# Loads on one queue, weight pieces by columns and a new order of issue, in a gated linear attention and MLP-mixer kernel

## The chip, the cores and the metric

The kernel runs on one core of one Trainium2 chip. A core has five engines with instruction streams of their own: PE (TensorE, matrix products), DVE (VectorE), ACT (ScalarE), POOL (GpSimd) and SP (SyncE, which here only issues transfers). They meet through semaphores. Sixteen DMA engines move data for all of them. The metric is the device time of one execution in microseconds (us); an execution of the profile has a span, which the time exceeds by what lies around it.

## The reference

The inputs are q, k, v and alpha, of shape 4 x 8 x 768 x 48 (batch, heads, positions, head width), and four weights. The first part is a recurrence with a state of 48 x 48 for each batch and head, the second a mixer over tokens and channels:

```python
for t in range(S):                       # S = 768
    state = alpha[:, :, t, :, None] * state + einsum('bhd,bhe->bhde', k[:, :, t], v[:, :, t])
    y[:, :, t] = einsum('bhd,bhde->bhe', q[:, :, t], state)
...
x = y.transpose(0, 2, 1, 3).reshape(B, S, H * D)         # 4 x 768 x 384
xt = x.transpose(0, 2, 1)
h = maximum(xt @ w_tok1, 0) @ w_tok2                     # 768 -> 256 -> 768
u = x + h.transpose(0, 2, 1)
out = u + maximum(u @ w_ch1, 0) @ w_ch2                  # 384 -> 1536 -> 384
```

## The kernel before

**Chunks.** The recurrence is cut into twelve chunks n of 256 positions, three to a batch (b = n // 3, k = n % 3). A chunk is loaded as four tiles of 128 partitions x 768 numbers (names ld_at, ld_kt, ld_qt, ld_vt with the number n; a partition holds two positions next to each other, so a run of memory is 384 bytes). Its steps, with the line that the profile shows: the logarithm of alpha (ln, L586, for chunks 0 to 2; P, ln1, lnP and r1 in the others, L577 to L589), its running sum by a triangular product on PE (cumw or cum), exponentials of plus and minus that sum (E, IE, Et), k times IE (kk) and q times E (qq, both L641; in chunks from 3 on after k0a, L633, and q0r, L637, which bring one of the two positions in), a copy of v to bf16 (vb) with two shifted halves (vs0, vs1) and, from chunk 3 on, shifted copies of k (ka, kb, kc). For chunks 0 to 5 PE transposes kk and qq (trk, trq, L654), and the results are copied out of PSUM (evk, evq); for the others a DMA transpose issued by SP does it (dk, dq, L665). Then G0 and G1 (products of k and q), the masks (L708), K (the new part of the state), s0, sa and sm (the state, L750, L753, L756), ia and ib (q with the state), y0 and y1 (the mask's result with v), x0 and x1 (the copy of y: a tile of 128 positions). On PE the products cum, K, G, ia, ib, y and the unread ones all go through one helper and show as L592.

**Mixer.** For each batch: t1 (first token weight, L790) with its relu ht, t2 (second token weight, L795; each t2_b_i makes 128 columns of h, i from 0 to 5), u = x + h (L799), transposes up of u with copies ut (batches 0 and 1) or DMA transposes ux (batches 2 and 3), c1_b_mc_half (first channel weight, L814; mc is one of twelve groups of 128 columns, half one of two groups of 384 positions, three matmuls each) with its relu rt on ACT (L785) or DVE (L787), c2_b_i_q4 (second channel weight, L819, four steps of three matmuls), o = u + result (L823) and the store st (L573). Of the last tile to finish, (3, 0), c2, o and st are done in two column ranges, h0 and h1.

**Weights.** Each weight is loaded in pieces of 128 x 768 float32 numbers (ldw_wt1, ldw_wt2, ldw_wc1, ldw_wc2 with the piece's number, L549 to L556), and cast to bf16 (cw_...). A step that reads a weight waits for the casts of the pieces that are named in its preds.

**Order.** Nothing is scheduled at run time. The string ORDER lists all steps with the engine that does each (t PE, s ACT, v DVE, g POOL, y SP), and the steps are emitted in that order, so each engine works its own through in order of the list; BUFS gives the buffers in the same order. Load tiles and weight pieces share twenty buffers of a class "in", o has four, PSUM eight banks. A step waits for what it reads and for the last reader of its buffer. Loads and stores may be issued by SP or ACT. One rule more: steps of DVE and POOL that are marked port=True (kk, qq, vb, vs, sm, P, k0a, q0r, ka, kb, kc, casts, pq) wait for the last such step of the other engine in the list's order (shared, L672 to L681).

**Unread products.** In the first three chunks a step may be preceded by fillers: f1_... is one product and f3_... are three products of a tile of zeros with itself, 128 x 512, written to the PSUM bank that the step then overwrites. Nothing reads them. Which of them are done is set by whether ORDER names them.

## Time and profile before

| | |
|---|---|
| median of three runs | 167.17 us (166.69 to 168.16) |
| the profiled execution | 167.49 us |
| its span | 165.8 us |
| moved by DMA | 34.46 MB in 74,530 packets, 67,984 of them under 512 bytes |
| read from and written to HBM | 25.17 MB and 4.72 MB |

A group of the profile has its line, engine, operation, what it writes and reads, the shape and the count, then the busy time in us and the mean ns of one, then the idle time of the engine just before such instructions and what ended most of it. A row of a timeline has the start in us, the time it covers, and in brackets the idle time before it and its releaser. The forty slices are a fortieth of the span each, some 4.1 us, and a digit is the busy share in tenths.

### The profile page before, as it was taken

To read this page: it belongs to the slowest core of one execution; us is meant where nothing else is said; L and a number is where in the kernel's file an instruction comes from. 1 tells how busy PE (TensorE), PEld (TensorE's weight loads), DVE (VectorE), ACT (ScalarE), POOL (GpSimd) and SP (SyncE) were. 2 spreads that over 40 slices of the span, in tenths; PEclk is the share of its full clock that TensorE was granted. 3 is DMA by queue.
4 is the path that set the end of the run, shared out by engine and by line. 5 is a ranking of instruction groups with operands and counts; after the bars stand their busy time and mean duration, and the time that the engine had idled before them with its cause. 6 is when DMAs were issued, how large, how long until landed. Compare 5 with 4: busy or idle time off the path is not lost. (4 is left out here: it accounts for less than half of the span.)

```text
span 165.8 us, 4057 instructions
## 1 busy us (share of the span) xinstructions
PE 155.9 (94%) x1606; PEld 99.2 (60%) x1606; DVE 117.6 (71%) x205; ACT 102.6 (62%) x195; POOL 65.3 (39%) x73
## 2 busy tenths in 40 slices
PE   7956999899889999999999999999999999999992
PEld 2434666576567666765567666666566565656662
DVE  4059999999769877997978899898584751353241
ACT  3685899999699974869988882846613203453000
POOL 4045966473294926386297584233020000000000
PEclk9999999999999999999999999999999999999999
DMA  4999999999999898999988999667601044150124
GB/s 116 323 325 324 320 325 369 373 321 335 368 353 315 204 298 208 271 264 190 303 237 129 241 270 144 142 134 163 185 0 51 0 90 100 47 190 4 47 95 142
DMA packets 74530, 34.46 MB, mean 208 GB/s; under 512 B 67984, under 2 KB 73488, under 8 KB 74512
## 3 DMA queue, kind: packets, MB, share of 16 engines
q1 hardware_dynamic: 58432, 25.47, 60.4%
q10 hardware_dynamic: 16080, 8.75, 17.9%
q8 instruction: 12, 0.20, 0.5%
q14 instruction: 6, 0.05, 0.1%
HBM read 25.17 MB, written 4.72 MB: 180 GB/s over the span
## 5 line engine op out<-in xcount | busy, mean ns | idle before, releaser
L819 PE MATMUL ps<-wc,rt 128*128 128x384 bf16 (+1 forms) x300 | 53.9, 320 | 0.0
L814 PE MATMUL ps<-ut,wc 128*128 128x384 bf16 x288 | 51.4, 326 | 1.7 <-ACT rt L785 1.6
L785 ACT ACTIVATE rt<-ps 128x384 bf16<-128x384 f32 x59 | 26.7, 490 | 21.4 <-PE ps L814 19.2
L814 PEld LDWEIGHTS <-wc 128*128 128x128 bf16 x288 | 27.3, 97 | 19.4 <-issue 2.4
L819 PEld LDWEIGHTS <-rt 128*128 128x128 bf16 x300 | 27.5, 97 | 15.5
L708 DVE TENSOR_TENSOR gtm<-ps,mk 128x1024 bf16<-128x1024 f32 x24 | 28.6, 1219 | 3.9 <-PE ps L592 3.5
L787 DVE TENSOR_SCALAR rt<-ps 128x384 bf16<-128x384 f32 x37 | 19.9, 554 | 11.0 <-PE ps L814 10.9
L823 DVE TENSOR_TENSOR o<-ps,u 128x384 f32<-128x384 f32 (+1 forms) x25 | 13.1, 536 | 11.8 <-PE ps L819 9.0
L641 POOL TENSOR_TENSOR pkk<-in,IE 128x768 bf16<-128x768 f32 x7 | 12.7, 1816 | 16.3 <-DVE pkk L641 7.7
L641 POOL TENSOR_TENSOR pkq<-in,E 128x768 bf16<-128x768 f32 x7 | 12.7, 1819 | 3.2 <-DVE ss L756 1.5
L592 PE MATMUL ps<-zs 128*128 128x512 bf16 x37 | 12.3, 454 | 1.6 <-DVE zs L495 1.1
L685 ACT CAST vb<-in 64x384 bf16<-64x384 f32 (+1 forms) x20 | 12.4, 621 | 1.1 <-DMA in<-in_v_dram 0.8
L685 ACT CAST x<-ps 128x384 bf16<-128x384 f32 x18 | 8.5, 476 | 7.4 <-PE ps L592 6.9
L799 DVE TENSOR_TENSOR u<-ps,x 128x384 bf16<-128x384 f32 x24 | 11.9, 550 | 1.3 <-PE ps L795 1.0
L756 POOL TENSOR_TENSOR ss<-tmp,E 128x384 bf16<-128x384 f32 x10 | 8.3, 835 | 7.8 <-DVE tmp L753 4.6
L577 POOL TENSOR_TENSOR in<-in 128x384 f32<-128x384 f32 x7 | 7.0, 1000 | 11.1 <-DVE wt L686 3.4
L790 PE MATMUL ps<-x,wt 128*128 128x384 bf16 x48 | 10.8, 326 | 0.3 <-ACT x L685 0.3
L753 DVE TENSOR_TENSOR tmp<-ps,ss 128x384 f32<-128x384 f32 x16 | 8.8, 553 | 2.0 <-PE ps L592 1.3
L641 DVE TENSOR_TENSOR pkk<-in,IE 128x768 bf16<-128x768 f32 x5 | 4.8, 954 | 7.1 <-ACT IE L625 6.0
L592 PE MATMUL ps<-tpq,tpk 48*64 48x128 bf16 (+1 forms) x288 | 8.5, 219 | 1.0 <-DVE tpq L686 0.8
L795 PE MATMUL ps<-ht,wt 128*128 128x384 bf16 x48 | 9.3, 326 | 0.0
L592 PEld LDWEIGHTS <-gtm 128*128 128x128 bf16 x192 | 7.6, 96 | 1.9
(93 smaller groups left out, 211.2 us busy)
## 6 DMA issues: line engine op xcount, KB each, us to landing
in<-in_q_dram SPq DMA_DIRECT2D x11, 384.0 KB, 5.1
in<-in_moe_w_ch_dram SPq DMA_DIRECT2D x10, 384.0 KB, 5.9
in<-in_alpha_dram SPq DMA_DIRECT2D x9, 384.0 KB, 5.8
in<-in_k_dram SPq DMA_DIRECT2D x9, 384.0 KB, 6.4
in<-in_v_dram SPq DMA_DIRECT2D x6, 384.0 KB, 5.5
in<-in_v_dram ACTq DMA_DIRECT2D x6, 384.0 KB, 5.7
out_dram<-o ACTq DMA_DIRECT2D x12, 192.0 KB, 2.6
out_dram<-o SPq DMA_DIRECT2D x11, 192.0 KB, 2.3
```

The source lines that it names most:

```text
L592: return self.pe.matmul(out, lhsT=lhsT, rhs=rhs, start=start, stop=stop, skip_group_check=True)
L641: self.shared(self.eng[e].tensor_tensor(self.t(dst)[:, :, :, 0:D], self.t(src).rearrange("p h s d -> p s h d"), bass.AP(tensor=f.tensor, o ...
L685: return self.act.copy(d, s)
L708: self.nc.vector.tensor_tensor(self.t(gtm)[:, hf, :, :], self.pair(gp).rearrange("p a (j t) -> p (a j) t", t=128), bass.AP(tensor=m.tensor ...
L785: self.act.activation(d, s, AF.Relu)
L787: self.nc.vector.tensor_scalar_max(d, s, 0.0)
L790: self.pe.matmul(self.bank(bank)[:, 0:HD], lhsT=self.wt1[:, kc, m * 128 : m * 128 + 128], rhs=self.t(x), start=(kc == 0), stop=(kc == NS - 1))
L795: self.pe.matmul(self.bank(bank)[:, 0:HD], lhsT=self.wt2[:, kc, i * 128 : i * 128 + 128], rhs=self.t(hts[kc]), start=(kc == 0), stop=(kc = ...
L799: self.nc.vector.tensor_tensor(self.t(u)[:, i % 3], self.bank(bank)[:, 0:HD], self.t(x), ALU.add)
L814: self.pe.matmul(self.bank(bank)[:, 0:HD], lhsT=self.wc1[:, kc, mc * 128 : mc * 128 + 128], rhs=self.t(ut)[:, 3 * half : 3 * half + 3, kc, ...
L819: self.pe.matmul(self.bank(bank)[:, 0 : cz - ca], lhsT=self.t(rts[mc][0])[:, i * 128 : i * 128 + 128], rhs=self.wc2[:, mc, ca:cz], start=( ...
L823: self.nc.vector.tensor_tensor(self.t(o)[:, ca:cz], self.bank(bank)[:, 0 : cz - ca], self.t(u)[:, i % 3, ca:cz], ALU.add)
```

## The change

Five things change. The computation stays the same.

- All loads are issued by SP. Before, ACT issued sixteen of the 64 loads and thirteen of the 25 stores; now it issues three stores.
- The second token weight is loaded in two halves of 384 columns (for all 256 rows) instead of two of 128 rows, and t2_b_i waits for the half that holds its columns instead of both.
- The first channel weight is loaded in six pieces of 256 columns (for all 384 rows) instead of six of 128 rows x 768 columns, and a c1 step waits for one piece instead of three. A run of memory is 1 KB instead of 3 KB, and 1.5 KB instead of 3 KB in the second token weight.
- The list names 23 unread products instead of 37.
- ORDER and BUFS are new as a whole, and with them the engine of many steps: without transfers, ACT has 173 steps instead of 194, DVE 197 instead of 187, POOL 72 instead of 61. The two ranges of the last tile are 320 and 64 columns instead of 192 each. (The fill that cum gets is empty, as cum is used from chunk 3 on only.)

The diff, with the part of the two lists that comes up to the first steps of c1 of batch 0:

```diff
@@ -162,7 +162,8 @@
             lnp = O("lnP", act(384, True), 1, writes=[la], reads=[at], preds=[p_], emit=lambda e: g.lnp(la, at))
             r1 = O("r1", act(384, True), 3, writes=[lf], preds=[ln1], emit=lambda e: g.r1(lf))
             cb = V("one")
-            cum = O("cum", pe([384] + [4] * 4 + [16]), 2, writes=[cb, E, IE], reads=[la], preds=[lnp], emit=lambda e: g.cum(cb, la))
+            cum = O("cum", pe([384] + [4] * 4 + [16]), 2, writes=[cb, E, IE], reads=[la], preds=[lnp] + fill("cumw", cb),
+                    emit=lambda e: g.cum(cb, la))
             e1 = et = O("E", act(400), 4, writes=[E], reads=[cb], preds=[cum], emit=lambda e: g.expE(E, cb))
             e2 = O("IE", act(384), 4, writes=[IE], reads=[cb], preds=[cum], emit=lambda e: g.expIE(IE, cb))
             k_in = [O("k0a", either(dve(384), pool_tt(384)), 2, writes=[kt], reads=[at], port=True,
@@ -290,7 +291,7 @@
                 u = V("u")
             bank = V("one")
             o = P.op(f"t2_{b}_{i}", pe([384] * 2), m0 + (1900 + 330 * i) * sc, writes=[bank],
-                     reads=[h for h, _ in hts], preds=[h for _, h in hts] + [wl[("wt2", p)] for p in range(2)],
+                     reads=[h for h, _ in hts], preds=[h for _, h in hts] + [wl[("wt2", i // 3)]],
                      emit=lambda e, i=i, bank=bank: g.tok2(bank, i, [h for h, _ in hts]))
             uo = P.op(f"u_{b}_{i}", dve(384), m0 + (1950 + 330 * i) * sc, writes=[u], reads=[bank, x[i][0]], preds=[o],
                       emit=lambda e, i=i, bank=bank, u=u: g.uadd(u, i, bank, x[i][0]))
@@ -319,7 +320,7 @@
             for half in range(2):
                 bank = V("one")
                 o = P.op(f"c1_{b}_{mc}_{half}", pe([384] * 3), m0 + (4900 + 975 * mc + 487 * half) * sc, writes=[bank],
-                         reads=[ut], preds=(uts[0:2 + half] if b in UP else [uts[half]]) + [wl[("wc1", mc // 6 * 3 + p)] for p in range(3)],
+                         reads=[ut], preds=(uts[0:2 + half] if b in UP else [uts[half]]) + [wl[("wc1", mc // 2)]],
                          emit=lambda e, mc=mc, half=half, bank=bank: g.ch1(bank, ut, mc, half))
                 ro.append(P.op(f"rt_{b}_{mc}_{half}", either(act(384), dve(384)),
                                m0 + (4950 + 975 * mc + 487 * half) * sc, writes=[rt], reads=[bank], preds=[o],
@@ -327,7 +328,7 @@
             rts.append((rt, ro))
         for i in range(NS):
             hold = 4000.0 if (i >= NS - 3 and b < B - 1) else 0.0
-            cuts = [(0, HD // 2), (HD // 2, HD)] if (b, i) == LAST else [(0, HD)]
+            cuts = [(0, 320), (320, HD)] if (b, i) == LAST else [(0, HD)]
             for ci, (ca, cz) in enumerate(cuts):
                 nm = f"{b}_{i}" if len(cuts) == 1 else f"{b}_{i}h{ci}"
                 bank, o_ = V("one"), V("o")
@@ -361,85 +362,84 @@
 
 ENGINES = {"t": "PE", "s": "ACT", "v": "DVE", "g": "POOL", "y": "SP"}
 ORDER = """
-f1_cumw0t ld_at1y f3_cumw1t f3_trk1t ld_at0s ld_kt1s f1_cumw1t ln1s f3_trq0t ld_kt0y ld_vt0y ld_qt0y ln0s ld_vt1y
-ld_qt1y ld_at2y cumw1t f1_K1t cumw0t ld_at3y E1s IE1s Et1s IE0s vb0s f1_K0t kk0v Et0s kk1g K0t f3_K1t s0_0v sa1_0v E0s
-qq0v vb1s trk0t sm1_0v f3_G00t trq0t ln2s trk1t evk0v ld_qt2y qq1g K1t evq0v evk1s sa0_1v ld_vt2s G0_0t cumw2t
-mask0_0v sm0_1g trq1t P3g ln13s E2s vs0_1s vs1_0s qq2g ld_kt3y ld_kt2y sa1_1v Et2s evq1v lnP3s f3_y0t f3_G01t IE2s
-G1_0t mask1_0v ib0t G0_1t f1_trq2t mask0_1v trq2t cum3t ld_qt3y k0a3g vs0_0g ldw_wt10y f3_G11t y1_0t ldw_wt11y y0_0t
-G1_1t evq2s ib1t ldw_wt21s f3_trk2t kk2v E3s IE3s trk2t sm1_1g mask1_1v vb2s vs1_1s f1_K2t ld_vt3y K2t evk2v G1_2t
-ldw_wt20y y1_1t ld_at4y sa0_2v f3_G02t kk3g x1_0s r13s sm0_2g q0r3g G0_2t mask1_2v vs0_2g cw_wt10s ia1t x0_0v y0_1t
-trk3t t1_0_1_0t mask0_2v ka3s ia2t ldw_wc14y t1_0_1_1t f1_y2t ib2t y0_2t vs1_2v kb3s ldw_wc15y y1_2t x1_1s cw_wt11s
-vb3v x0_1s t1_0_1_2t t1_0_0_0t t1_0_1_3t kc3s x0_2s t1_0_1_4t vs0_3v vs1_3v ldw_wc13y x1_2s t1_0_0_1t qq3v cw_wt21s
-t1_0_0_2t t1_0_1_5t cw_wt20v t1_0_0_3t t1_0_0_4t t1_0_0_5t ht_0_1s K3t trq3t ld_kt4y ht_0_0s P4g s0_3v sa1_3v t2_0_2t
-t2_0_3t evk3s sm1_3g t2_0_0t t2_0_1t t2_0_5t ldw_wc12y ldw_wc10y ldw_wc11y u_0_3v u_0_2v u_0_0v up_0_1t t2_0_4t evq3s
-lnP4s cw_wc14g cw_wc15g u_0_1v ib3t ut_0_1s ln14s ld_kt5s u_0_5v cw_wc13g up_0_0t cum4t ld_at5y E4s G0_3t IE4s u_0_4v
-G1_3t k0a4g ut_0_0v up_0_2t c1_0_10_0t mask0_3v c1_0_9_0t ut_0_2s rt_0_10_0s rt_0_9_0s mask1_3v c1_0_7_0t c1_0_9_1t
-c1_0_6_0t c1_0_10_1t c1_0_8_0t c1_0_8_1t cw_wc12s y1_3t cw_wc10s rt_0_10_1s kk4v rt_0_7_0v cw_wc11v rt_0_6_0v trk4t
-c1_0_1_0t P5g ka4g c1_0_4_1t rt_0_8_1v c1_0_1_1t k0a5g ld_vt4s r14s x1_3s c1_0_3_1t c1_0_0_0t evk4v rt_0_1_1v
-rt_0_0_0v rt_0_8_0s ln15s ldw_wc20s lnP5s rt_0_4_1s rt_0_3_1s ld_qt4y cum5t c1_0_2_0t kc4v kb4s ldw_wc24s IE5s
-rt_0_9_1s c1_0_11_1t q0r4v qq4v c1_0_4_0t ld_vt5s rt_0_1_0s rt_0_2_0v E5s c1_0_2_1t rt_0_4_0s rt_0_11_1s kk5g
...
+f1_cumw0t f3_cumw0t ld_at0y ld_vt0y vb0v ld_at1y ln0s cumw0t ld_kt0y ld_qt0y ld_at2y ln1s IE0s f1_trq1t f1_cumw1t
+ld_at3y Et0s kk0v E0s cumw1t ld_qt1y K0t qq0v ld_vt1y IE1s ld_kt1y s0_0v sa1_0v trk0t vs1_0v ld_qt2y evk0v Et1s ln2s
+E1s vs0_0s P3g trq0t cumw2t evq0s f3_G00t f1_G10t ld_vt2y G0_0t f3_G10t IE2s lnP3s ld_kt2y f1_trk1t G1_0t qq1v sm1_0v
+mask0_0v mask1_0v Et2s ld_kt3y ldw_wt10y ld_vt3y ldw_wt20y ldw_wt11y trq1t vb1g kk1g ldw_wt21y K1t E2s y0_0t cum3t
+evq1s trk1t f3_y0t sa0_1v evk1s ln13s vs1_1s E3s IE3s qq2v sm0_1v x0_0v ld_at4y sa1_1v G0_1t mask0_1v ib0t y1_0t kk2g
+f1_trq2t G1_1t ld_qt3y trq2t ldw_wc12y r13s ld_kt4y ldw_wc14y mask1_1v vs0_1s trk2t x1_0v f1_y1t vb2s evk2v k0a3g
+sm1_1g ldw_wc15y evq2s K2t sa0_2v f3_y1t cw_wt10s G0_2t vb3s ib1t y1_1t ldw_wc10y G1_2t ia1t ia2t t1_0_1_0t mask0_2v
+t1_0_1_1t y0_1t kk3g ld_qt4y vs1_2g sm0_2g cw_wt11g cw_wt21g kb3s vs0_2s y0_2t trk3t x0_1s mask1_2v t1_0_0_0t
+t1_0_0_1t x1_1v ka3s x0_2s vs1_3s vs0_3s t1_0_1_2t ldw_wc21y f1_y2t ib2t t1_0_0_2t t1_0_1_3t kc3s ldw_wc11y evk3v
+t1_0_0_3t t1_0_0_4t y1_2t x1_2s K3t t1_0_1_4t P4v cw_wt20v ld_at5y ldw_wc13y lnP4s q0r3v t1_0_1_5t s0_3v t1_0_0_5t
+ht_0_0s ld_kt5y ht_0_1v ldw_wc23y sa1_3v cum4t t2_0_0t t2_0_1t ln14s u_0_0v ld_vt4y qq3g u_0_1v ld_vt5y t2_0_2t
+cw_wc12g trq3t IE4s t2_0_3t t2_0_4t u_0_2v t2_0_5t up_0_0t ldw_wc20y E4s u_0_3v evq3s up_0_1t k0a4g ldw_wc22y u_0_4v
+ib3t u_0_5v cw_wc14g kk4g G1_3t ut_0_1v mask1_3v ut_0_0s r14s G0_3t cw_wc10s cw_wc15s up_0_2t c1_0_5_0t c1_0_9_0t
+mask0_3v ld_qt5y ut_0_2v y1_3t c1_0_4_0t trk4t evk4s ka4s kb4g q0r4g sm1_3g ldw_wc24y x1_3v cw_wc21g rt_0_9_0v
+c1_0_1_0t ldw_wc25y qq4g c1_0_8_0t c1_0_0_0t y0_3t c1_0_11_0t kc4g rt_0_5_0v rt_0_0_0v cw_wc13g c1_0_10_1t c1_0_11_1t
+ld_at6y c1_0_0_1t k0a5g P5g cw_wc23g vb4g x0_3s cw_wc11s rt_0_1_0s rt_0_0_1v c1_0_10_0t rt_0_11_0v rt_0_4_0v
+rt_0_10_1s vb5g trq4t c1_0_8_1t c1_0_7_1t c1_0_2_0t rt_0_8_1v evq4s ln15s c1_0_4_1t c1_0_9_1t c1_0_6_1t vs1_4g
...
 """
 BUFS = """
...
 """
@@ -548,10 +548,11 @@
             w = self.w[0].rearrange("(c p) m -> p c m", p=128)
             self.gated(dma(t.rearrange("p (c m) -> p c m", c=3), w[:, 3 * piece : 3 * piece + 3, :]), op)
         elif nm == "wt2":
-            self.gated(dma(t, self.w[1][128 * piece : 128 * piece + 128, :]), op)
+            w = self.w[1].rearrange("(c p) m -> p c m", p=128)
+            self.gated(dma(t.rearrange("p (c m) -> p c m", c=2), w[:, :, 384 * piece : 384 * piece + 384]), op)
         elif nm == "wc1":
-            h, c = divmod(piece, 3)
-            self.gated(dma(t, self.w[2][128 * c : 128 * c + 128, 768 * h : 768 * h + 768]), op)
+            w = self.w[2].rearrange("(c p) m -> p c m", p=128)
+            self.gated(dma(t.rearrange("p (c m) -> p c m", c=3), w[:, :, 256 * piece : 256 * piece + 256]), op)
         else:
             self.gated(dma(t.rearrange("p (c m) -> p c m", c=2),
                            self.w[3][256 * piece : 256 * piece + 256, :].rearrange("(c p) m -> p c m", p=128)), op)
@@ -561,10 +562,9 @@
         if nm == "wt1":
             d, t = self.wt1[:, 3 * piece : 3 * piece + 3, :], t.rearrange("p (c m) -> p c m", c=3)
         elif nm == "wt2":
-            d = self.wt2[:, piece, :]
+            d, t = self.wt2[:, :, 384 * piece : 384 * piece + 384], t.rearrange("p (c m) -> p c m", c=2)
         elif nm == "wc1":
-            h, c = divmod(piece, 3)
-            d = self.wc1[:, c, 768 * h : 768 * h + 768]
+            d, t = self.wc1[:, :, 256 * piece : 256 * piece + 256], t.rearrange("p (c m) -> p c m", c=3)
         else:
             d, t = self.wc2[:, 2 * piece : 2 * piece + 2, :], t.rearrange("p (c m) -> p c m", c=2)
         self.copy(e, d, t)
```

More of the change, by code (lines that the diff above doesn't have):

```diff
@@ new lines @@
+q0r7v qq7g vs0_7g sa1_6v st_0_2y st_0_1y dk7y r18s rt_1_11_1s cum8t c1_1_5_1t c1_1_4_1t ld_vt8y ld_at10y o_0_3v
+rt_1_7_0v rt_1_0_1v o_0_4v c1_1_2_0t pq6s rt_1_5_1s c1_1_2_1t c1_1_10_1t q0r8v ld_kt8y rt_1_2_0v sm1_6g vs1_7s ka7g
+kc7g ln19s E8s c1_1_5_0t kb7g rt_1_6_0s c1_1_1_1t c1_1_9_0t rt_1_10_1v c1_1_3_1t ld_vt10y rt_1_5_0v rt_1_4_1v
+rt_1_2_1v c1_1_0_0t lnP9s rt_1_1_1s IE8s rt_1_3_1s ld_kt11y ld_qt9y dq7y st_0_4y cum9t ln110s ld_kt10y c1_1_8_1t
+rt_1_0_0s rt_1_8_1s K7t IE9s E9s P10v k0a8v c1_1_8_0t c1_1_3_0t c1_1_6_1t rt_1_3_0s qq8v c1_1_11_0t c1_1_7_1t
@@ new lines @@
+rt_2_11_0s t2_3_3t t2_3_2t t2_3_5t c2_2_0_0t u_3_2v u_3_3v t2_3_4t c2_2_4_2t c2_2_0_1t c2_2_2_0t t2_3_0t u_3_5v u_3_4v
+c2_2_3_1t c2_2_0_2t c2_2_0_3t c2_2_4_3t c2_2_1_0t c2_2_3_2t t2_3_1t o_2_4v ux_3_1y c1_3_2_1t rt_3_2_1s c1_3_10_1t
+rt_3_10_1s c2_2_2_1t c2_2_2_2t c1_3_6_1t u_3_0v u_3_1v rt_3_6_1v c1_3_4_1t c2_2_3_3t c2_2_1_1t c1_3_0_1t ux_3_0y
+st_2_4y c2_2_1_2t c1_3_1_1t c2_2_2_3t o_2_0v c1_3_5_0t c1_3_1_0t o_2_3v rt_3_1_1v c1_3_0_0t rt_3_5_0v rt_3_1_0s
+rt_3_4_1s rt_3_0_1v c1_3_2_0t c1_3_5_1t c1_3_8_0t rt_3_2_0s o_2_2v c1_3_3_1t c1_3_9_1t rt_3_0_0v rt_3_9_1v st_2_0y
```

87 lines of the change are left out of this document (38 added, 49 removed), and 22 rows, old and new, of the table BUFS.

## The prediction

> **What bounds the kernel now.** I read the page first (the forty slices), then the busy time by stretch, then the timeline of each engine over the first 52 us, and the chain of waits last.
>
> ```profile
> PE   7956999899889999999999999999999999999992
> ...
> GB/s 116 323 325 324 320 325 369 373 321 335 368 353 315 204 298 208 271 264 190 303 237 129 241 270 144 142 134 163 185 0 51 0 90 100 47 190 4 47 95 142
> ```
>
> PE is full from about the tenth slice on; before that it has gaps, and in those slices the transfers run flat at 320 to 325 GB/s. So there are two stages with different limits. The busy time by stretch (PE, PEld, DVE, ACT, POOL, clock, DMA, GB/s) says which engines are full in the first:
>
> ```profile
> 12.00:36.00 24.00, 21.99 (x317) 14.82 (x314) 23.23 (x34) 20.96 (x37) 16.79 (x18) 1.00 1.08 339
> 36.00:52.00 16.00, 14.79 (x147) 9.79 (x145) 13.40 (x20) 14.06 (x28) 8.67 (x9) 1.00 1.13 346
> 52.00:163.00 111.00, 110.15 (x1087) 70.34 (x1083) 76.93 (x133) 60.61 (x122) 36.30 (x35) 1.00 0.68 158
> ```
>
> From 12 to 36 us DVE works 23.23 of 24 us: the front is bound by DVE, by its fixed order, and by the loads that it waits for. From 52 us on PE works 110.15 of 111 us. PE's timeline where they meet:
>
> ```profile
> 35.69 4.07 PE L814 MATMUL ps<-ut,wc 128*128 128x384 bf16 x24
> 39.59 0.36 PE L592 MATMUL ps<-vb,gtm 128*128 128x48 bf16 x8
> 39.80 0.61 PE L654 MATMUL ps<-idn,pkk 128*128 128x128 bf16 x8
> 40.24 2.60 PE L814 MATMUL ps<-ut,wc 128*128 128x384 bf16 x15
> ```
>
> The first channel product (c1, L814) of batch 0 starts at 35.69. Counted from the two lists of order, the useful products behind that point are the same ones before and after (all of t1, t2 and up of batch 0, and of chunk 3 all but its y, stand ahead of it in both). So the time of the changed kernel is the old one, plus the shift of the start of c1, plus the change of PE's waits behind it, plus the change of the tail. Work saved on PE ahead of c1 counts only through that start.
>
> **The fewer unread products.** The list has 37 products of the zero tile before and 23 after, 14 fewer.
>
> ```profile
> L592 PE MATMUL ps<-zs 128*128 128x512 bf16 x37 | 12.3, 454 | 1.6 <-DVE zs L495 1.1 <-ACT IE L625 0.5
> ```
> ```profile
> 1.06 4.88 PE L592 MATMUL ps<-zs 128*128 128x512 bf16 x11 [1.06 <-DVE zs L495]
> ...
> 17.23 1.46 PE L592 MATMUL ps<-zs 128*128 128x512 bf16 x6
> ```
>
> The first row is their group with its count, the others stand in PE's timeline. The six at 17.23 take near 0.22 us each, less the last one's drain; the eleven at 1.06 take 0.44 each. So 14 are worth 3 to 6 us of PE, all ahead of c1, where PE isn't the limit. I cost them at nothing: their cover is the waiting in the front; if PE were the limit there, their going would be a gain.
>
> **The start of c1.** Loads first. Their arrival shows where an engine's wait ends on one:
>
> ```profile
> 11.75 0.83 ACT L685 CAST vb<-in 128x768 bf16<-128x768 f32 x1 [0.77 <-DMA in<-in_v_dram]
> ```
> ```profile
> 21.67 0.96 DVE L641 TENSOR_TENSOR pkk<-in,IE 128x768 bf16<-128x768 f32 x1 [0.24 <-DMA in<-in_k_dram]
> ```
>
> The cast at 11.75 waits for the seventh load, and 393 KB at 325 GB/s is 1.21 us. The slices show the same rate where ACT issues as well and where SP does alone, so SP alone puts the n-th load near 11.75 + 1.21 (n - 7): the first alpha at 4.5, chunk 1's k, now tenth instead of among the first four, at 15.4, chunk 2's k, thirteenth, at 19.0 instead of 21.67. The column pieces cut the runs: 3 KB to 1 KB for the channel weight, 3 KB to 1.5 KB for the token weight. Their price is bounded by stretches in which such runs move (1 KB pieces of the first token weight, then 3 KB pieces):
>
> ```profile
> 22.00:23.00 1.00, 1.00 (x17) 0.54 (x11) 1.00 (x2) 1.00 (x3) 0.23 (x1) 1.00 1.05 361
> 33.00:34.00 1.00, 0.86 (x13) 0.69 (x13) 1.00 (x4) 0.93 (x3) 1.00 (x3) 1.00 1.03 387
> ```
>
> 393 KB at 361 against 387 GB/s is 1.09 against 1.02 us, 0.44 us for six pieces, nothing to 0.44 of it in the time: the first two pieces (22nd and 24th load) land by 32 by the rule above, ahead of their use, so I take nothing.
>
> Now the steps. The groups with their mean ns:
>
> ```profile
> L641 POOL TENSOR_TENSOR pkk<-in,IE 128x768 bf16<-128x768 f32 x7 | 12.7, 1816 | 16.3 <-DVE pkk L641 7.7 <-DVE pkq L641 6.7 <-DVE in L633 1.1
> L756 POOL TENSOR_TENSOR ss<-tmp,E 128x384 bf16<-128x384 f32 x10 | 8.3, 835 | 7.8 <-DVE tmp L753 4.6 <-DVE pkk L641 1.5 <-DVE in L577 1.3
> L577 POOL TENSOR_TENSOR in<-in 128x384 f32<-128x384 f32 x7 | 7.0, 1000 | 11.1 <-DVE wt L686 3.4 <-DVE wc L686 3.3 <-DVE pkk L686 3.1
> L633 POOL TENSOR_TENSOR in<-in,in 128x384 f32<-128x384 f32 x6 | 6.0, 1004 | 2.2 <-DVE ss L756 2.1
> L686 POOL CAST wc<-in 128x768 bf16<-128x768 f32 x5 | 4.0, 825 | 0.0
> ```
> ```profile
> L686 POOL CAST vb<-in 64x384 bf16<-64x384 f32 x7 | 3.5, 498 | 7.4 <-PE ps L795 4.2 <-DVE vb L686 2.6 <-DVE kt L686 0.4
> ```
> ```profile
> L708 DVE TENSOR_TENSOR gtm<-ps,mk 128x1024 bf16<-128x1024 f32 x24 | 28.6, 1219 | 3.9 <-PE ps L592 3.5
> ...
> L823 DVE TENSOR_TENSOR o<-ps,u 128x384 f32<-128x384 f32 x23 | 12.4, 552 | 11.0 <-PE ps L819 9.0 <-DMA out_dram<-o 2.0
> L799 DVE TENSOR_TENSOR u<-ps,x 128x384 bf16<-128x384 f32 x24 | 11.9, 550 | 1.3 <-PE ps L795 1.0
> L753 DVE TENSOR_TENSOR tmp<-ps,ss 128x384 f32<-128x384 f32 x16 | 8.8, 553 | 2.0 <-PE ps L592 1.3
> L641 DVE TENSOR_TENSOR pkq<-in,E 128x768 bf16<-128x768 f32 x5 | 4.8, 957 | 0.2
> ```
> ```profile
> L686 DVE COPY tpk<-ps 128x1024 bf16<-128x1024 bf16 x3 | 2.1, 685 | 0.1
> ```
> ```profile
> L685 ACT COPY tpq<-ps 128x1024 bf16<-128x1024 bf16 x3 | 4.0, 1321 | 0.3 <-PE ps L654 0.3
> ```
> ```profile
> L685 ACT COPY ut<-ps 128x768 bf16<-128x768 bf16 x2 | 1.6, 798 | 0.2 <-PE ps L806 0.2
> ```
>
> And six of them in a row in DVE's timeline, which shows what a hand-over saves:
>
> ```profile
> 32.10 2.88 DVE L799 TENSOR_TENSOR u<-ps,x 128x384 bf16<-128x384 f32 x6
> ```
>
> Chunk 1's kk is still on POOL, now behind the load: 15.45 + 1.82 = 17.3, then K1's sixteen products (about 0.5, between the 0.36 and the 0.61 of the rows of eight at 39.59 and 39.80) and the state's add sa0_1 on DVE from about 17.85. DVE then does sa0_1, qq2 and sm0_1 (0.55, 0.96, 0.55, less 0.07 for each, as those six took 2.88 where six means of 0.55 make 3.3) to 19.75. Steps of DVE and POOL that share the port wait for each other in the list's order, so POOL starts there: kk2 1.82, k0a3 1.00, sm1_1 0.84, kk3 1.82, vs1_2 0.50, sm0_2 0.84, two weight casts at 0.83: 8.5 us, with eight hand-overs of some 0.05 us 28.6. DVE meanwhile has four masks (4.88), five steps of 0.55 and two copies at 0.69, together 9.0 less 0.8, to 28.0, and must wait at P4 until 28.6. Behind that stand six steps of 0.55, the six u adds (2.88) and one copy of ut, 6.3 us, and some 0.3 of hand-over: 35.2. P4, a weight cast and q0r3, 0.48 each, end at 30.1. On ACT the copy ut_0_0 stands behind evq3, which needs qq3, now on POOL behind q0r3: 30.15 + 1.82 + transposes 0.6 + evq3 1.3 + ut 0.8 with hand-overs gives 34.9. c1 starts at about 35.3: **0.4 us earlier**. The ends: 33.2, if the front follows chunk 2's k (21.67 to 35.69 is 14.0 us; 19.0 and 14.0 make 33.0), and 38, if port and POOL run as late as under the third rival. I take the value of the steps, since DVE's row of 23.23 in 24 says that work, not the load, fills the front.
>
> **The waits behind it.** The one long wait of PE between 36 and 52, in PE's timeline and then in ACT's:
>
> ```profile
> 46.29 0.65 PE L814 MATMUL ps<-ut,wc 128*128 128x384 bf16 x3 [1.21 <-ACT rt L785]
> ```
> ```profile
> 45.33 0.37 ACTq L533 DMA_DIRECT2D in<-in_v_dram  x1
> 45.75 0.49 ACT L785 ACTIVATE rt<-ps 128x384 bf16<-128x384 f32 x1 [1.45 <-DMA in<-in_v_dram]
> ```
>
> ACT was held 1.45 us by a load that it had to issue, with evictions queued behind it. With 26 issues moved to SP (some 0.37 us each, 9.6 us of ACT) this goes: minus 1.21. What is late next: the chunk 3 product y1_3 is third in c1's row on PE and needs a mask that DVE begins only behind ut_0_1 (35.2 + 1.2 = 36.4, PE is there at 36.3): 0.1 us. And c1_0_7_1 needs the fourth column piece, whose cast is POOL's twelfth step from qq3 on: 3 x 1.82 + 4 casts at 0.83 + 2 x 1.00 + 0.84 + 2 x 0.5 = 12.6, hand-overs 0.6, from 30.15 to 43.3. PE is there after 12 products of 0.49 (24 matmuls between 35.69 and 39.59 are 3.90 us), two y at 0.21, two transposes at 0.44: 42.5. Wait 0.8. Together minus 1.21 plus 0.9, **minus 0.3**; ends minus 1.2 and plus 1.5 (a wait like the old one for each of the two late casts). From 52 us on PE idles 0.85 us in 111, so there is little to win; I take nothing, with minus 0.8 and plus 1.5. SP is what could lose there: all stores and the DMA transposes stand in one queue with the loads, and a store behind a waiting transpose keeps one of four o tiles; loads, though, run 20 tiles ahead in both lists.
>
> **The tail.** The last piece to finish is now 320 columns wide instead of 192.
>
> ```profile
> L823 DVE TENSOR_TENSOR o<-ps,u 128x192 f32<-128x192 f32 x2 | 0.7, 358 | 0.8 <-issue 0.6
> ```
> ```profile
> out_dram<-o SPq DMA_DIRECT2D x11, 192.0 KB, 2.3
> ```
> ```profile
> out_dram<-o SPq DMA_DIRECT2D x1, 96.0 KB, 1.6
> ```
>
> Against the add of 384 columns (0.552) and the store of 192 KB the piece grows by two thirds of the difference: 0.13 for the add, at most 0.47 for the store, of which I take a third, as most stores in that row had others beside them; **plus 0.3**. The two parts of the product are together as wide as before.
>
> **Sum.** Minus 0.4, minus 0.3, plus 0.3: minus 0.4 on the profiled execution's 167.49, 167.1; the median of the runs, 167.17, lies 0.3 below that execution, so I give 166.8.
>
> **Rivals.** *The front follows the loads* (c1 at 33.2): minus 2.5, minus 1.2 and plus 0.3 on 167.49 make 164.1, on the median 163.8. For it: kk2 at 21.67 did wait for its load, and 3 us of unread products go; against: DVE had no idle time to give back. *The front is held by chunk 3's q* (slower): qq3 goes from DVE (0.96) to POOL (1.82), behind the shared port, and evq3 stands on ACT ahead of ut_0_0 and, through G1_3 and G0_3, on PE ahead of the last up and of c1. Each hand-over that costs 0.15 rather than 0.05, over some 20 of them between kk1 and evq3, moves it 2 us, and a late load of chunk 3's q (21st, due at 28.2: ten loads at 1.21 and four weight pieces at 1.09 behind the seventh) moves it one for one. c1 at 38 gives plus 2.3, minus 0.3, plus 0.3: 169.8, on the median 169.5. It decides from c1 at 37.4 on, 1.7 us late. *The clock starts cold*: the eleven unread products at 1.06 ran at half the pace of the six at 17.23; only four are left at the start, with a gap to the first logarithm behind them, so the first sums, K0 and transposes may run at 0.44 to 0.22. That is up to 1.3 us on G0_0, of which mask1_0 in front of sa0_1 passes on 0.9: 168.0, on the median 167.7.
>
> [...]
>
> **Chances.** One per cent, 1.7 us, is about what a measurement of this kernel can tell from no change. The forecast 0.36 (0.33 within 1%, 0.03 faster); the loads' front 0.29, faster; chunk 3's q 0.27, slower; the cold clock 0.08 (0.06 within, 0.02 slower). Faster 0.32, same 0.39, slower 0.29. The range runs from the loads' front to c1 at 38, with 0.2 and 0.4 for what else differs: 163.6 to 169.9; the forecast's own is 165.9 (none of the 0.9 of new waits) to 168.3 (1.5 more behind 52).
>
> **What would show it.** c1 (L814) starting at 35.3 on PE; ACT without a wait on a load among its evictions from 36 to 52; POOL's kk1 beginning at 15.4, kk2 at 19.8; POOL's casts done when PE asks for the fourth piece, or a wait of some 0.8 near 42.5; the last add at 0.49 us; the same 110 of 111 us behind 52. It would be wrong if c1 starts before 34 or after 37.4, if PE has new waits past 52 that end on SP's stores or transposes, or if early products show half pace past 12 us.

## The result, and the profile after

The new kernel takes 166.26 us (median of 20 runs, 165.60 to 168.25), the kernel before, run beside it, 167.93 us (20 runs, 166.69 to 168.30): a ratio of 0.9902, 95% interval 0.9887 to 0.9918. The forecast was 166.8 us. The ratios in this document leave out the runs in a slower state of the chip, so they can differ by some tenths of a per cent from the quotient of the medians.

The profiled execution of the new kernel took 167.10 us, span 165.4. That lies 0.84 above its median, while the profiled execution of before, 167.49, lies 0.44 below the median of the 20 runs. So the two traces show 0.39 of the 1.67 us between the medians; they tell where time moved, and the runs tell how much. Only one of the new kernel's 20 runs took longer than its profiled execution, so what each step took in a median one isn't known.

The busy time by stretch (PE, PEld, DVE, ACT, POOL, clock, DMA, GB/s):

```profile
12.00:36.00 24.00, 19.97 (x292) 13.23 (x290) 20.44 (x33) 20.59 (x35) 16.31 (x16) 1.00 1.10 322
36.00:52.00 16.00, 15.90 (x145) 10.05 (x142) 12.97 (x25) 12.36 (x23) 12.20 (x14) 1.00 1.08 335
52.00:162.00 110.00, 109.49 (x1095) 69.69 (x1092) 78.15 (x136) 55.20 (x107) 42.54 (x43) 1.00 0.68 162
```

DVE works 20.44 of 24 us in the front, where it had worked 23.23: the front isn't filled by DVE's work any more, yet it doesn't end earlier. From 36 to 52 us PE works 15.90 of 16 us instead of 14.79. The last stretch was and is PE's.

PE's timeline at the points that the forecast named:

```profile
32.12 1.15 PE L795 MATMUL ps<-ht,wt 128*128 128x384 bf16 x6 [0.97 <-ACT IE L622]
...
36.36 1.14 PE L814 MATMUL ps<-ut,wc 128*128 128x384 bf16 x6
...
43.04 3.85 PE L814 MATMUL ps<-ut,wc 128*128 128x384 bf16 x21
...
154.77 7.34 PE L819 MATMUL ps<-wc,rt 128*128 128x384 bf16 x56
```

c1 starts at 36.36, 0.67 later than the 35.69 of before. The last matmul ends at 154.77 + 7.34 = 162.11, so from c1's start to there it takes 125.75 us. Before, that end was at 162.72:

```profile
154.81 7.91 PE L819 MATMUL ps<-wc,rt 128*128 128x384 bf16 x58
```

That made 127.03 us, so 1.28 are gained behind the start. The wait of 1.21 us for a held ACT is gone, and where a wait for the fourth column piece was forecast there is a small one: POOL's cast of that piece, and the sum over PE's waits for POOL's casts, from the page's costliest groups (the weight load, PEld, is what waits).

```profile
42.91 0.83 POOL L686 CAST wc<-in 128x768 bf16<-128x768 f32 x1
```
```profile
L814 PEld LDWEIGHTS <-wc 128*128 128x128 bf16 x288 | 27.2, 98 | 17.5 <-POOL wc L686 0.5
```

By the records of the two traces PE's idle time behind the start of c1 falls from 1.72 us (1.21 at 46.29, 0.39 at 118.66, 0.12 at 80.25) to 0.43 (0.10 at 43.79, which is that cast's, and 0.33 at 95.10).

What held the start, in DVE's timeline and then in POOL's:

```profile
30.57 0.56 DVE L637 TENSOR_TENSOR in<-in,lf 128x384 f32<-128x384 f32 x1 [1.06 <-DMA in<-in_q_dram]
...
31.51 0.55 DVE L787 TENSOR_SCALAR ht<-ps 128x384 bf16<-128x384 f32 x1
...
162.15 0.49 DVE L823 TENSOR_TENSOR o<-ps,u 128x320 f32<-128x320 f32 x1 [0.66 <-PE ps L819]
```
```profile
15.16 1.81 POOL L641 TENSOR_TENSOR pkk<-in,IE 128x768 bf16<-128x768 f32 x1
19.92 1.82 POOL L641 TENSOR_TENSOR pkk<-in,IE 128x768 bf16<-128x768 f32 x1 [2.95 <-DMA in<-in_k_dram]
...
31.21 1.81 POOL L641 TENSOR_TENSOR pkq<-in,E 128x768 bf16<-128x768 f32 x1 [2.93 <-DVE in L637]
```

DVE stands 1.06 us at q0r3 for chunk 3's q. Behind it in DVE's order stands the relu ht_0_1 at 31.51, and t2 (L795) starts at 32.12, when that is done; on POOL qq3 waits for q0r3. (The page puts PE's wait down to IE, whose end falls on the same 32.12; t2 doesn't read it. It starts 0.05 to 0.06 behind ht_0_1's end in the traces of three variants too.) The other half of the relu, ht_0_0, on ACT, was ready 0.73 us earlier, at 31.33:

```profile
30.84 0.49 ACT L785 ACTIVATE ht<-ps 128x384 bf16<-128x384 f32 x1 [0.17 <-PE ps L790]
```

The landing times of the sixteen parts (rings) of the load of that q, sorted, from the trace:

```
chunk 3's q: 27.87 27.90 27.92 28.05 28.08 28.18 28.21 28.27 28.32 28.35 28.39 28.40 28.40 28.55 29.30 30.55
```

Fourteen are there by 28.55, and the semaphore is complete with the last, at 30.55.

### The profile page after: what moved, and what is told of

It reads as the page before. It is cut to its first block, busy times and chain, and to the rows that moved or that the text cites. A ratio compares the mean times of both kernels' runs of the same rounds, so it can differ in the third digit from the quotient of the medians.

```text
span 165.4 us, 4033 instructions
## 1 busy us (share of the span) xinstructions
PE 153.3 (93%) x1592; PEld 97.1 (59%) x1592; DVE 118.3 (72%) x215; ACT 95.2 (58%) x174; POOL 73.4 (44%) x84
## 5 line engine op out<-in xcount | busy, mean ns | idle before, releaser
L819 PE MATMUL ps<-wc,rt 128*128 128x384 bf16 (+2 forms) x300 | 54.9, 319 | 0.0
L785 ACT ACTIVATE rt<-ps 128x384 bf16<-128x384 f32 x49 | 22.2, 490 | 26.1 <-PE ps L814 25.8
L787 DVE TENSOR_SCALAR rt<-ps 128x384 bf16<-128x384 f32 x47 | 24.2, 552 | 11.0 <-PE ps L814 10.7
L823 DVE TENSOR_TENSOR o<-ps,u 128x384 f32<-128x384 f32 (+2 forms) x25 | 13.3, 537 | 13.1 <-PE ps L819 11.4
L641 POOL TENSOR_TENSOR pkk<-in,IE 128x768 bf16<-128x768 f32 x8 | 14.5, 1818 | 3.2 <-DMA in<-in_k_dram 2.9
L686 POOL CAST vb<-in 64x384 bf16<-64x384 f32 (+1 forms) x13 | 8.1, 625 | 8.4 <-issue 4.4
L685 ACT CAST x<-ps 128x384 bf16<-128x384 f32 x13 | 6.2, 476 | 9.1 <-PE ps L592 7.0
L577 POOL TENSOR_TENSOR in<-in 128x384 f32<-128x384 f32 x6 | 6.0, 1003 | 11.3 <-DVE vb L686 8.9
L795 PE MATMUL ps<-ht,wt 128*128 128x384 bf16 x48 | 9.6, 326 | 1.0 <-ACT IE L622 1.0
L685 ACT COPY tpq<-ps 128x1024 bf16<-128x1024 bf16 x6 | 7.9, 1314 | 3.6 <-PE ps L654 3.5
L592 PE MATMUL ps<-zs 128*128 128x512 bf16 x23 | 7.7, 442 | 2.2 <-ACT tpq L685 1.2
```

The source lines that it names most:

```text
L592: return self.pe.matmul(out, lhsT=lhsT, rhs=rhs, start=start, stop=stop, skip_group_check=True)
L641: self.shared(self.eng[e].tensor_tensor(self.t(dst)[:, :, :, 0:D], self.t(src).rearrange("p h s d -> p s h d"), bass.AP(tensor=f.tensor, o ...
L685: return self.act.copy(d, s)
L785: self.act.activation(d, s, AF.Relu)
L787: self.nc.vector.tensor_scalar_max(d, s, 0.0)
L795: self.pe.matmul(self.bank(bank)[:, 0:HD], lhsT=self.wt2[:, kc, i * 128 : i * 128 + 128], rhs=self.t(hts[kc]), start=(kc == 0), stop=(kc = ...
```

## The experiments

Where an expectation names a theory by a letter: A, ACT was held by the issue of its own load, and that is what the change gets back behind c1's start; B, the start of c1 follows the late q of chunk 3; C, the column pieces bring something of themselves; D, the unread products at the start set the granted clock.

**Five loads from ACT to SP.** In the kernel before, those that ACT issued between 33 and 46 us:

```diff
-ld_kt5s
-ld_vt4s
-ldw_wc20s
-ldw_wc24s
-ld_vt5s
+ld_kt5y
+ld_vt4y
+ldw_wc20y
+ldw_wc24y
+ld_vt5y
```

> The old kernel with five loads of its stage from 33 to 46 us (chunk 5's k, chunk 4's v, chunk 5's v, first and fifth piece of the second channel weight) issued by SP instead of ACT, at the same place in the list. Theory A (the gain comes from ACT no longer being held by a load among its evictions): PE's 1.2 us wait near 46 us goes, 1.0 to 1.4 us faster than before, ratio 0.992 to 0.994. Theory B (the gain comes from the front: fewer unread products, another order): no change, ratio 0.998 to 1.002. Theory C (column pieces): no change.

Measured: 167.79 us, ratio 1.0008 (0.998 to 1.0036). ACT's hold is gone, and nothing is gained. PE's timeline, DVE's and SP's:

```profile
47.16 0.62 PE L688 MATMUL ps<-idn,pkq 128*128 128x128 bf16 x8 [1.33 <-DVE pkq L675]
```
```profile
45.55 0.56 DVE L671 TENSOR_TENSOR in<-in,lf 128x384 f32<-128x384 f32 x1 [1.57 <-DMA in<-in_q_dram]
```
```profile
38.86 0.37 SPq L567 DMA_DIRECT2D in<-in_v_dram  x1
...
39.91 0.46 SPq L567 DMA_DIRECT2D in<-in_q_dram  x1
```

Chunk 4's v has to wait for its buffer until 38.86, and now that wait stands in SP's queue: chunk 4's q, issued at 32.89 in the kernel before, is issued at 39.91 and lands at 45.46, and the transposes of q wait. The stall only moved.

**One load from ACT to SP.** Only the load that held ACT:

```diff
-ld_vt5s
+ld_vt5y
```

> The kernel before with one load alone moved: chunk 5's v (ld_vt5) is issued by SP, between its loads of chunk 4's and chunk 5's q, instead of by ACT, which stood at that issue among its evictions. Theory A (ACT held by its own load is the price that the new kernel gets back): the wait of 1.36 us before c1_0_5_1 falls below 0.4, the time from the start of c1 to the last matmul falls by 0.8 to 1.2 us from 127.0, the median by as much: ratio 0.993 to 0.996. Rival (the hold covers another lateness, as in the run with five loads moved, where a wait of 1.49 us came 0.7 us later): a wait of over 0.8 us stands elsewhere between 42 and 50 us, ratio 0.998 to 1.002.

Measured: 166.53 us, ratio 0.9927 (0.9898 to 0.9955). ACT's evictions run through, and the wait is nearly gone:

```profile
43.35 2.89 PE L848 MATMUL ps<-ut,wc 128*128 128x384 bf16 x15
46.08 0.61 PE L688 MATMUL ps<-idn,pkq 128*128 128x128 bf16 x8
```
```profile
44.67 0.87 ACT L819 ACTIVATE rt<-ps 128x384 bf16<-128x384 f32 x2
45.41 0.53 ACT L653 ACTIVATE E<-ps 128x400 f32<-128x400 f32 x1
45.79 0.91 ACT L819 ACTIVATE rt<-ps 128x384 bf16<-128x384 f32 x2
```

Fifteen products take 2.89 us here, 2.60 where they run without a gap. From the start of c1 to the last matmul it takes 126.24 us in this trace, 0.79 less than before: the one long wait is gone, and small ones (0.12 to 0.23) are left. So theory A has its price, some 1.2 us by the runs (0.75 to 1.7), where what waits behind the load in its new queue isn't due yet:

```profile
34.61 3.48 SPq L567 DMA_DIRECT2D in<-in_v_dram  x1
38.15 1.55 SPq L567 DMA_DIRECT2D in<-in_q_dram  x1
```

SP stands 3.48 us at this issue, with chunk 5's q behind it. With five loads moved, it was chunk 4's q that stood behind a waiting issue, and what was gained was paid back.

**All sixteen loads from ACT to SP**, in the old order (the suffix s to y for each of them):

> The old kernel with all sixteen loads of ACT issued by SP, at the same places in the list; stores stay where they were. Theory A: as with the five loads, 1.0 to 1.4 us faster, and no more than 0.5 us beyond that either way, as the other eleven loads held nobody for long. Theory B: the two alphas now come one behind the other, chunk 0's first and then chunk 1's or the reverse, so the front moves by at most 0.5 us; no gain. Theory C: no change.

Measured: 169.37 us, ratio 1.0108 (1.006 to 1.0155). DVE's timeline and PE's, far behind the front:

```profile
120.91 0.56 DVE L720 CAST vb<-in 128x768 bf16<-128x768 f32 x1 [3.49 <-DMA in<-in_v_dram]
```
```profile
121.99 0.32 PE L853 MATMUL ps<-wc,rt 128*128 128x384 bf16 x1 [2.24 <-DVE rt L821]
```

The last v is issued by SP behind its DMA transposes, at 114.50, and lands at 120.81; DVE waits for it with evictions queued behind. (This trace, of mean clock 0.988, also has a stretch of half clock, of which the last section tells.) So all loads on SP cost 1% in the old order, which the new order had to win back.

**Column pieces alone**, in the kernel before:

```diff
-[wl[("wt2", p)] for p in range(2)]
+[wl[("wt2", i // 3)]]
...
-[wl[("wc1", mc // 6 * 3 + p)] for p in range(3)]
+[wl[("wc1", mc // 2)]]
```

with the loads and casts of these pieces as in the new kernel.

> The old kernel with the column pieces alone (second token weight in two halves of 384 columns, first channel weight in six pieces of 256 columns), the list of order unchanged. Theories A and B: no change, since the first channel product found its pieces cast before; at most 0.4 us slower by the shorter runs. Theory C: 1 us or more faster.

Measured: 167.42 us, ratio 0.9963 (0.9933 to 0.9993): some 0.6 us gained, though its wait before c1_0_5_1 is still there (1.66 us in its trace).

**Column pieces and chunk 5's v together**, the two edits above in one:

> The kernel before with both parts that gained when done alone: the weights in column pieces (0.9963) and chunk 5's v issued by SP (0.9927). If they take off two different waits, the gains add: ratio 0.987 to 0.991, as much as the whole change (0.9902), and the new issue order and the fewer unread products are worth nothing together. If both free the same wait before c1_0_5_1: ratio 0.992 to 0.995, and what is left of the change's gain comes from the new order.

Measured: 166.00 us, ratio 0.9900 (0.9872 to 0.9928). The gains add: 0.9963 times 0.9927 is 0.9890. Its stretches:

```profile
36.00:52.00 16.00, 15.96 (x157) 10.47 (x156) 14.67 (x23) 15.04 (x31) 8.61 (x9) 1.00 1.12 344
52.00:161.00 109.00, 108.76 (x1074) 69.58 (x1071) 75.46 (x129) 59.60 (x119) 36.33 (x35) 1.00 0.66 162
```

PE is as full from 36 us on as in the new kernel, with ACT still issuing fifteen loads, all 37 unread products and the old order but for one step. These two edits make as much as the whole change.

**Fourteen fewer unread products**, in the kernel before:

```diff
-f3_G01t
-f3_G11t
-f3_trk2t
-f3_G02t
-f1_K2t
-f1_trq2t
```

> The old kernel without fourteen of its unread products, those between 17.9 and 25.6 us (the three before G0 and G1 of chunk 1, before chunk 2's transpose of k and its G0, and one each before K and the transpose of q of chunk 2). Theory A: no change within 0.4 us, PE isn't the limit there. Theory B: 0.7 us or more faster.

Measured: 167.97 us, ratio 1.0002 (0.9975 to 1.003). They cost nothing where they stood.

**Four unread products at the start instead of eleven**, in the kernel before:

```diff
-f3_trk1t
-f1_cumw1t
-f3_trq0t
```

> The kernel before with seven of its eleven early unread products left out (f3_trk1, f1_cumw1, f3_trq0; nobody reads them), so that TensorE begins with four, as in the new kernel. Theory D (early unread products raise the granted clock at 4 us, and it falls back for 3.4 us in the gap after them, in some executions): no execution has a mean clock below 0.995, the record reads full clock from about 8 us on without a stretch of one half, start of c1 within 0.5 us of 35.7, and the median is lower by about the share of disturbed executions times their price, 11 of 29 times 0.56 = 0.2 us: ratio 0.997 to 1.0. Rival (the stretch of half clock is the chip's own and doesn't hang on these products): about 4 of 10 executions have it, ratio 0.999 to 1.003.

Measured: 169.54 us, ratio 1.0101 (1.0059 to 1.0143). The stretch of half clock that theory D speaks of didn't come in six runs (no mean clock under 0.995; the last section tells of it), but where the theory gave a small gain there is a cost of 1%. PE's timeline:

```profile
6.01 1.12 PE L626 MATMUL ps<-la,u 128*128 128x384 bf16 x3 [3.06 <-ACT la L620]
...
7.91 1.17 PE L626 MATMUL ps<-la,u 128*128 128x384 bf16 x3
8.87 0.53 PE L626 MATMUL ps<-la,us 128*128 128x384 bf16 x1
```

Three products of the running sum take 1.17 us, ahead of the clock's rise at 9.68 in this trace, and stand behind those of chunk 1; in the kernel before, behind the rise at 5.97, they took 0.65:

```profile
7.09 0.65 PE L592 MATMUL ps<-la,u 128*128 128x384 bf16 x3
```

The sum of chunk 0 is done at 9.62 instead of 8.12, and c1 starts at 36.84, 1.15 later than in the trace of before. In the old order the early products are worth some 1.7 us by the runs (1.0 to 2.4).

**Eleven unread products at the start of the new kernel**, ten instead of three in its second early run:

```diff
-g.fill(bank, z)
+g.fill(bank, 10 if nm == "cumw0" and z == 3 else z)
```

> The new kernel with ten products instead of three in its second early run (f3_cumw0), so eleven early unread products as the kernel before has. Theory D: some 3 to 5 of 10 executions have a mean clock below 0.995, full clock from about 4 us and one half between about 11 and 14 us; the median is 0.1 to 0.6 us above the new kernel's 166.26. Rival: no execution below 0.995, and the median within 0.2 of 166.26.

Measured: 167.16 us (12 runs), ratio 0.9955 (0.9925 to 0.9984). Two of twelve runs had a mean clock under 0.995, fewer than theory D's three to five in ten. Against one in 42 of the new kernel and its variants with the same start this leans to theory D and doesn't decide it. The first product that follows the sum of chunk 0 (K0) comes at 9.30 us, not before the 9.18 of the new kernel: it waits for kk0 on DVE. So in the new order, whose alpha of chunk 0 lands at 4.16 instead of 5.77 us, no cost of the later rise of the clock (8.29 us in the new kernel's trace) shows. Why the ten other runs too are some 0.8 above the new kernel's median (they weren't run beside it) stays open; the trace shows no place for it.

**One piece of the token weight behind chunk 3's q**, in the new kernel, on SP, and its cast on DVE behind q0r3:

```diff
-ldw_wt20y ldw_wt11y ldw_wt21y ld_at4y ld_qt3y
+ldw_wt11y ldw_wt21y ld_at4y ld_qt3y ldw_wt20y
...
-P4v cw_wt20v ld_at5y ldw_wc13y lnP4s q0r3v
+P4v lnP4s q0r3v cw_wt20v ld_at5y ldw_wc13y
```

(The first two lines leave out the steps of other engines between the loads.)

> The new kernel with one piece of the second token weight (ldw_wt20) behind chunk 3's q instead of ahead of it on SP, and its cast on VectorE behind the product that needs that q (q0r3). Theory B (chunk 3's q, landing at 30.55 instead of the forecast 28.2, is what put the start of c1 at 36.4 instead of 35.3): its last ring lands one piece earlier, at 29.5 to 29.9, q0r3 begins there, c1 begins at 35.3 to 35.8, and the median is 165.4 to 165.9, ratio 0.984 to 0.988. Rival (the token stage's own chain holds c1, or the weight's cast now holds the second token products): c1 at 36.0 or later with a wait before t2_0_0 of over 1 us, ratio 0.989 to 0.993.

Measured: 166.09 us, ratio 0.9891 (0.9862 to 0.9920), and c1 starts at 36.40. DVE's timeline and POOL's:

```profile
29.48 0.55 DVE L671 TENSOR_TENSOR in<-in,lf 128x384 f32<-128x384 f32 x1
30.61 0.56 DVE L720 CAST wt<-in 128x768 bf16<-128x768 f32 x1 [0.58 <-DMA in<-in_moe_w_tok_dram]
...
31.56 0.55 DVE L821 TENSOR_SCALAR ht<-ps 128x384 bf16<-128x384 f32 x1
```
```profile
31.25 1.82 POOL L675 TENSOR_TENSOR pkq<-in,E 128x768 bf16<-128x768 f32 x1 [2.78 <-DVE wt L720]
```

q0r3 came 1.09 us earlier, as expected, and the weight's cast took its place: DVE waits for that load until 30.61, ht_0_1 stands at 31.56 as before, and qq3 waits for the cast, which the turn of the steps marked port=True puts ahead of it. This is the rival's second half, the weight's cast in the place of the q, and the ratio lies in its range (though PE's wait before t2 is 0.48 us, not the rival's 1). The edit put a new late load where the old one had been, so it doesn't decide on theory B.

**The other piece behind it instead**, with its cast on POOL behind qq3, and the last tile cut 192 and 192:

```diff
-ldw_wt21y ld_at4y ld_qt3y
+ld_at4y ld_qt3y ldw_wt21y
...
-cw_wt21g
...
-qq3g
+qq3g cw_wt21g
...
-cuts = [(0, 320), (320, HD)]
+cuts = [(0, HD // 2), (HD // 2, HD)]
```

> The new kernel with the second piece of the second token weight (ldw_wt21) behind chunk 3's q on SP instead of two places ahead of it, in an input buffer that is free until 44 us, and its cast on GpSimd behind qq3; the other piece and its cast on VectorE stay ahead, so that no cast with the shared port stands between q0r3 and qq3 (in the run with ldw_wt20 behind the q one did: q0r3 began 1.1 us earlier, and qq3 waited for that cast's end, 31.17, and began at 31.25 as before). The last output tile is cut 192 and 192. Theory B: chunk 3's q has landed by 29.5, q0r3 follows the cast that ends at about 29.5, qq3 begins at 30.1 to 30.4 instead of 31.2, and c1 at 35.6 to 36.0, now behind ht_0_0; minus 0.4 to 0.7 for the start and minus 0.28 for the tail, median 165.2 to 165.7, ratio 0.982 to 0.987. Rival (c1's start doesn't hang on this q): c1 within 0.2 us of 36.2, only the tail is gained, 165.8 to 166.1, ratio 0.987 to 0.991.

Measured: 166.16 us, ratio 0.9930 (0.9892 to 0.9968); c1 at 36.39. POOL's timeline, DVE's, ACT's and PE's:

```profile
15.94 1.81 POOL L675 TENSOR_TENSOR pkk<-in,IE 128x768 bf16<-128x768 f32 x1 [0.45 <-DMA in<-in_k_dram]
...
30.84 1.82 POOL L675 TENSOR_TENSOR pkq<-in,E 128x768 bf16<-128x768 f32 x1 [2.65 <-DVE in L671]
```
```profile
30.21 0.55 DVE L671 TENSOR_TENSOR in<-in,lf 128x384 f32<-128x384 f32 x1
```
```profile
31.62 0.49 ACT L819 ACTIVATE ht<-ps 128x384 bf16<-128x384 f32 x1 [0.17 <-PE ps L824]
```
```profile
32.16 1.14 PE L829 MATMUL ps<-ht,wt 128*128 128x384 bf16 x6 [0.22 <-ACT ht L819]
```

q0r3 waits for no load any more (the q landed at 28.70). But in this execution chunk 1's k landed at 15.80 instead of 15.03, kk1 began at 15.94 instead of 15.16, and the whole chain behind it, to the relu ht_0_0, is 0.78 later: it ends at 32.11 instead of 31.33, and t2 waits for that. So the expectation fell: the start wasn't gained. It shows the second chain, 0.73 us behind the first in the trace of the new kernel (31.33 against 32.06, the end of ht_0_1). The three executions of the new kernel and its variants in which the q alone was late stand one for one. From each trace:

```
kernel                      q landed   q0r3 began   c1 began   c1 - landing
new kernel                     30.55        30.57      36.36           5.81
last tile cut 192 and 192      30.22        30.25      36.04           5.82
eleven unread products         30.41        30.43      36.22           5.81
```

In the last two kk1 began 0.11 to 0.13 later than in the new kernel, and c1 still came 0.14 to 0.32 earlier, with the q.

**The last tile cut 192 and 192**, in the new kernel:

```diff
-cuts = [(0, 320), (320, HD)]
+cuts = [(0, HD // 2), (HD // 2, HD)]
```

> The new kernel with its last output tile cut 192 and 192 again instead of 320 and 64. By the forecast's tail term (320 columns: plus 0.3): the last add falls from 0.49 us to about 0.3, and from the last matmul to the end of the span it takes 3.0 instead of 3.29 us. Rival (the tail is the store's own latency, and the narrower add is given back by a later first piece): 3.2 to 3.4 us.

Measured in one run: 166.64 us, span 164.9. DVE's timeline and PE's:

```profile
161.97 0.36 DVE L857 TENSOR_TENSOR o<-ps,u 128x192 f32<-128x192 f32 x1 [0.18 <-PE ps L853]
```
```profile
154.75 7.18 PE L853 MATMUL ps<-wc,rt 128*128 128x384 bf16 x55
```

The last matmul ends at 161.93, and from there it is 3.0 us to the end of the span; in the new kernel 165.4 less 162.11, 3.3.

**This cut, and the piece of the token weight behind the q:**

> The same, and the last output tile cut 192 and 192 as in the kernel before. By the tail term (minus 0.23 to 0.28, the tail was 3.01 with this cut and 3.29 without) it is 0.2 to 0.3 below the run with the load alone: 165.1 to 165.7, ratio 0.982 to 0.987. Rival (what the start gains is given back at the waits behind 43 us): ratio 0.988 to 0.991, with waits behind c1 of over 2.5 us in all instead of 1.8.

Measured: 165.74 us, ratio 0.9870 (0.9844 to 0.9897), the lowest of all. It is 0.35 below the same edit without the cut, run beside it. Against the new kernel the intervals still touch (0.9887 to 0.9918), so that it beats both kernels is likely and not shown.

## Why the prediction came out as it did

The time, 166.26, lies 0.5 below the forecast; the sum of the forecast on the profiled execution, minus 0.4, is also what the pair of traces shows. But it is so by terms that were off in both directions, so that the sum came this close is in part luck.

**The start of c1, forecast at 35.3 (minus 0.4), came at 36.36 (plus 0.67).** This step failed. Its early part held in its times: kk1 began at 15.16 (forecast 15.4), kk2 at 19.92 (19.8), P4 at 28.49 (28.6). For kk2 that was luck: the forecast had POOL wait for DVE there, with chunk 2's k in at 19.0, but DVE was done at 19.47, and POOL waited for that k, whose last ring landed at 19.76. What failed is the rule that puts the n-th load at 11.75 + 1.21 (n - 7), with chunk 3's q due at 28.2. Its median ring was there at 28.3, its last at 30.55, and q0r3, which waits for it, began at 30.57. The kernel before shows such a lag too: its chunk 2's k, whose wait the prediction shows at 21.67, had its first ring at 19.87 and its last at 21.55. This is the mechanism of the second rival, "a late load of chunk 3's q moves it one for one", which the three executions above show, at about 1 us instead of the rival's 2.7. Without it, as an estimate from these rows, the start would have followed the chain through chunk 1's k and ht_0_0: 0.73 earlier, 35.63. The other 0.3 would then be that the forecast added up the steps of DVE and did not follow PE's t1 products, for which ht waits. So in the trace of after both ways of the front hang on the last ring of a load, and DVE, which the forecast took for the bound, has time left.

**The waits behind it, forecast minus 0.3, came out at minus 1.28.** The minus 1.21 for ACT's hold was right, and the run with one load moved shows it alone: 1.23 us by its ratio. The plus 0.9 of new waits was mis-sized: PE's records have 0.10 (0.26 over the usual pitch of its starts) at the fourth column piece and none at y1_3. The late q isn't what shortened this wait, since it moved both sides alike: POOL's twelve steps from qq3 on began 1.06 later than forecast (31.21 against 30.15), and so did c1. What was off is how long those steps take: the cast was done at 43.74 (forecast 43.3), 12.53 us behind the start of qq3 instead of 13.15, as the hand-overs, put at 0.6, cost nothing in POOL's rows. PE was there at 43.53 (forecast 42.5). The small waits behind 52 us, put at nothing, gave another 0.18.

**The tail, plus 0.3:** right, 3.29 against 3.06 us, and 3.01 with the old cut.

**The unread products, nothing:** right for the fourteen between 17.9 and 25.6 us. The seven at the start are another matter: in the old order they were worth 1.0 to 2.4 us (ratio 1.0101 without them), in the new one the clock rises at 8.3 us and no cost of that shows (K0 at 9.18, and at 9.30 with seven more of them), which is the third rival's condition without its price. The 12 us up to which the prediction allowed half pace was its author's estimate and no run shows it; in the four clock records of the last section full clock first begins at 4.07 to 9.68 us.

**The column pieces' shorter runs, nothing:** no price showed, and a gain of 0.37% (0.07 to 0.67%) that the forecast didn't have. In which wait it lies the traces don't show: between the two runs with chunk 5's v on SP, without and with column pieces, waits of 0.13 at 45.6, 0.23 at 52.7 and 0.19 at 118.3 us go.

**The new order and all loads on SP.** The forecast treated them as the change's core. The two small parts together make 0.9900, the whole change 0.9902: the rest nets to nothing that can be told, with 0.3 of it lost in the tail, and, as far as the old order tells, 1% to be won back first because SP alone issues the loads.

## What to carry to other kernels

Before a step that issues a transfer is moved to another engine, look at what that issue itself waits for, and at what will then stand behind it: moving the one load that held ACT gained 0.7%, moving five gained nothing, and moving all sixteen lost 1%. A load's due time from a mean rate was here that of its middle ring (28.2 against 28.3 us, with the last at 30.55), so put a margin of a ring's lag (here, for loads that land from 18 to 46 us, the last ring came 0.8 to 2.3 us behind the middle one) on the one load that a chain ends on, and see that no cast with a later load stands in the same queue ahead of the step. When two engines' rows begin at the same load, a lateness of that load moves both (here POOL's row by 1.06 us, and c1's with it), and a wait between them hangs on the length of their own steps.
